# A maximum over partitions by two TensorE transposes instead of GpSimd's partition instruction

## The chip, the core and the metric

The kernel runs on one core of a Trainium2 chip. The metric is the time of one execution on the device in microseconds, the median of three runs. A core has five engines with a queue of instructions each: TensorE (PE in the rows: matrix products and transposes, results in PSUM banks), VectorE (DVE), ScalarE (ACT: functions by tables, copies), GpSimd (POOL) and SyncE (SP, which issues the transfers here).

## The reference

Linear attention with a softmax of q over the head dimension and of k over the tokens, and then two gated layers:

```python
k_s = k - np.max(k, axis=2, keepdims=True)          # k: 8 batches, 8 heads, 576 tokens, 64
k_s = np.exp(k_s)
k_s = k_s / (np.sum(k_s, axis=2, keepdims=True) + 1e-09)
kv = np.einsum('bhsd,bhse->bhde', k_s, v)
x = np.einsum('bhsd,bhde->bhse', q_s, kv)           # q_s: the same softmax over q's last axis
...                                                 # x becomes 4608 tokens x 512
x = (sigmoid(x @ w_gate) * (x @ w_val)) @ w_out     # d_ff 1536
h = x @ w_in                                        # d_ff 2048
g = (a[0] + a[1]*h + a[2]*h**2 + a[3]*h**3) / (1 + abs(b[0])*abs(h) + abs(b[1])*h**2 + 1e-6)
out = g @ w_out2
```

The maximum of k runs over the tokens, and in the kernel the tokens of a block lie on the 128 partitions: one maximum for each of the 128 columns of a pair of heads.

## The kernel before, in words

Tokens go in 9 blocks of 512 (`j`). The first layer is a loop over blocks and over 12 slices of the hidden dimension (`f`); one pass is a step. A step has on TensorE the front (`front_a`: 24 products of three-pass float32, into `pg` and `pv`) and the back of the step before (`back_a`: 12 products into four accumulators). ScalarE takes the sigmoid of `pg`, VectorE multiplies it with `pv` (`sg`), and the product is split in a high and a low part (`gh`, `gl`). The second layer follows in the same manner and reads the first layer's result from DRAM.

The attention of block `j` is spread over the steps of the block before, in four units (`u`, a pair of heads each). A unit at step `d` of its block (`UNIT_STEPS` 4, 6, 8, 10) has: at `d-4` the maximum of k over the 5 tokens of each partition (`att_km`, VectorE), then the maximum over the partitions (`partition_all_reduce` on GpSimd, `kma`) and the subtraction (`att_ks`, VectorE); at `d-3` the exponentials (`att_ke`, `att_qe`, ScalarE; they need another table than the sigmoid, so a table is loaded each way); at `d-2` the normalization of q (`att_n`, VectorE); at `d-1` the kv products (`att_kv`) and the four transposes of q (`att_q`); at `d` their product (`att_d`). The steps `d-1`, `d-3` are odd and `d`, `d-2`, `d-4` even, so two units share a step. The results of kv, of the transposes of q and of `att_d` rotate through the two PSUM banks of `ps_x`: each takes the bank of the one before the last, and waits until that has been read.

The opening is made otherwise: the first block's attention and layer, the second block's attention and the way in of the weights (float64 words, made float32 and split, on ScalarE, VectorE and GpSimd) are listed as operations with costs (`KINDS`), and a list scheduler (`in_time`) writes them out in the order that these costs suggest. The costs only set the order in each queue. In the opening most subtractions of k and q are on GpSimd, and so are the low parts of the weights (`wl`) and of `gl`.

Of the kernel before, what the change touches and what calls it, by code (L numbers as in the profile page):

```python
# [10 lines left out]
F32 = mybir.dt.float32  # L11
F32R = mybir.dt.float32r
U32 = mybir.dt.uint32
AF = mybir.ActivationFunctionType
# [5 lines left out]
P = 128  # L20
# [16 lines left out]

# The kinds of operations of the first block: engine, weight, table of the scalar engine. They only order the emission.
PE, ACT, DVE, POOL, DMA = "PE", "ACT", "DVE", "POOL", "DMA"
KINDS = {  # L40
    "load_k": (DMA, 0.92), "load_q": (DMA, 0.74), "load_v": (DMA, 0.92), "load_w": (DMA, 1.46), "load_ab": (DMA, 0.06),
    "k_max": (DVE, 0.73), "k_all": (POOL, 1.3), "k_sub": (POOL, 1.5), "k_exp": (ACT, 0.63, "exp"),
    "q_max": (DVE, 0.6), "q_sub": (POOL, 1.0), "q_exp": (ACT, 0.63, "exp"),
# [15 lines left out]
def in_time(ops, on_dve):  # L59
    """List scheduling: yields the operations in the order in which the engines can start them; an engine takes,  # L60
    of what is ready, the one with the longest rest behind it."""
    followers = {o: [] for o in ops}
# [42 lines left out]
def kernel(ctx: ExitStack, tc: tile.TileContext, q, k, v, w1, w2, ab_in, out):  # L105
    """Every float32 product is three float32r passes: an operand is H + L, where H is its value
    rounded to 12 bits and L the exact rest, and the product is H*H + L*H + H*L."""
    nc = tc.nc
# [49 lines left out]
    def order(last):  # L158
        """Four sums of three passes: those with the last operand to arrive at the end, or sum by sum."""
        return [(m, n) for m in range(4) for n in range(3)] if last else [(m, n) for n in range(3) for m in range(4)]  # L160

    stage = stage_ctx.enter_context(tc.tile_pool(name="stage", bufs=STAGES))

# [1 line left out]
    # in the order of their use: the last third of a step's with the next step's  # L165
    order1 = [x for f in range(NF1 + 1) for x in [(f, 0), (f, 1), (f - 1, 2)] if 0 <= x[0] < NF1]
# [21 lines left out]

    # float64 and float32 agree in the sign and in the exponent's top bit and low 7 bits for every
    # magnitude of float32; those beyond are first brought to the words of zero and infinity.  # L190
    def prep_bits_a(p):
# [22 lines left out]
    def prep(until, times=1):  # L214
        """Moves up to `until` pieces through the last stage, and those behind them one stage on."""
        for _ in range(times):
            jobs = []
            for n in (4, 3, 2, 1, 0):
                ready = done[n - 1] if n else len(pieces)
                if n == 0 and done[0] - done[3] >= STAGES:  # L220
                    continue
                if done[n] < min(ready, until + (4 if n == 0 else 3 if late_pool and n < 4 else 0)):
                    jobs.append((prep_load, prep_abs, prep_bits_a, prep_bits_b, prep_split)[n](done[n]))
                    done[n] += 1
            yield from mix(*[x for x in jobs if x])
# [9 lines left out]
    def run(*jobs):  # L235
        """Emits the jobs' operations in turn, so that an engine seldom waits for the operation before."""
        jobs = list(jobs)
        while jobs:
            for x in list(jobs):
                if next(x, jobs) is jobs:  # L240
                    jobs.remove(x)
# [6 lines left out]

# [1 line left out]
    att = att_ctx.enter_context(tc.tile_pool(name="att", bufs=2))  # L250
# [18 lines left out]
    def att_km(j, u):  # L269
        km = att.tile([P, P], F32, tag="km", name="km")  # L270
        nc.vector.tensor_reduce(out=km, in_=kt[j, u].rearrange("p c d -> p d c"), axis=AX.X, op=ALU.max)  # L271
        yield
        kmt[j, u] = att.tile([P, P], F32, tag="kma", name="kma")
        nc.gpsimd.partition_all_reduce(kmt[j, u], km, P, bass_isa.ReduceOp.max)  # L274

# [91 lines left out]

# [1 line left out]
    accs = {}  # L369
# [36 lines left out]

# [1 line left out]
    # The first block, with the weights' way in and the second block's attention: what each operation has to follow  # L408
    # because of its operands or of the room that it writes. Half of the first units use room that is free till then.
    free = x_raw.rearrange("p m c -> p (m c)")  # L410
# [9 lines left out]
    def chain(names, gen, *after):  # L420
        """Operations that a generator emits one after another."""
        for name in names:
            op(name, lambda: next(gen, None), *after)
            after = (name,)
# [9 lines left out]
    for i in range(2 * NHP):  # L434
# [8 lines left out]
        op(n("load_v"), partial(load_v, j, u), n("kv", 1 if j and u else 2), n("load_v", 1))  # L443
        chain([n("k_max"), n("k_all")], att_km(j, u), n("load_k"), n("k_max", 1), n("k_all", 2))
        also(n("k_all"), n("k_sub", 2), n("k_all", 1))
        op(n("k_sub"), partial(att_ks, j, u, pool_or_dve(n("k_sub"))), n("k_all"))
        op(n("q_max"), partial(att_qm, j, u), n("load_q"), n("q_max", 1), n("q_sub", 3))
# [8 lines left out]
        if j == 0:  # L456
            chain([n("x"), n("x_h"), n("x_l")], att_d(j, u), n("kv_l"), n("qt_l"))
            banks += [n("x")] if u == NHP - 1 else [("kv", 0, u + 1), ("qt", 0, u + 1), n("x")]
        else:
            chain([n("xa"), n("xa_out"), n("xb"), n("xb_out")], att_d(j, u), n("kv_l"), n("qt_l"),  # L460
                  *[("kv", 0, i) for i in range(1, NHP)])
            banks += [n("kv"), n("qt"), n("xa"), n("xb")]
    # the two rotating banks of the attention, in the order of their use
    last = {"kv": "kv_l", "qt": "qt_l", "x": "x_l", "xa": "xa_out", "xb": "xb_out"}
    for a, b in zip(banks, banks[1:]):
# [46 lines left out]

    work = {}

# [3 lines left out]
    for j in range(2, NBLK):  # L518
        for u in range(NHP):
# [4 lines left out]
            if j < B:  # L524
                at(d - 4, att_km, j, u)
                at(d - 4, att_ks, j, u, nc.vector)
                at(d - 3, att_ke, j, u)
                at(d - 3, load_v, j, u)
                at(d - 1, att_kv, j, u)
            at(d - 4, att_qm, j, u)  # L530
            at(d - 4, att_qs, j, u, nc.vector)
            at(d - 3, att_qe, j, u)
            at(d - 2, att_n, j, u, nc.vector)
# [15 lines left out]
    for i in range(NF1, NA):  # L549
# [11 lines left out]
        if f == NF1 - 1:  # L561
            split_x()
        want = 0
        if j == NBLK - 2:
# [4 lines left out]
        if pend:  # L569
            back_a(*pend.pop(0))  # L570
        pend.append((j, f))
        if j == NBLK - 1 and f == 4:
# [4 lines left out]

# [1 line left out]
    while done[4] < NW:  # L579
# [143 lines left out]
```

## Time and profile before

| what | us |
|---|---|
| median of three runs (1906.37 to 1907.53) | 1906.66 |
| span of the profiled execution, first to last instruction | 1899.6 |
| time of a run outside of that span | 7.1 |
| busy TensorE in the span | 1777.8 |
| busy VectorE, ScalarE, GpSimd | 1218.2, 997.4, 367.4 |

The profile shows one execution with the span given. Busy times are sums over the whole span; where an engine is full and where it waits is read from the stretches and timelines below.

### The profile page before, as it was taken

What the parts mean: (1) busy time and instruction counts of PE and PEld (TensorE: products, weight loads), DVE (VectorE), ACT (ScalarE), POOL (GpSimd) and SP (SyncE); (2) the same over time, 40 slices, a digit from 0 to 9 for tenths busy, and PEclk for the clock granted to TensorE, in tenths of its full rate; (3) what the DMA queues carried; (4) which work ended last, traced back from release to release, by engine and by line L of the source; (5) the groups of instructions that cost most, each with busy time, mean ns of one, the idle gap of its engine ahead of it and who ended that gap; (6) DMA issues with size and microseconds to landing.
All of it is one profiled execution on the core that took longest, in us unless ns stands there. A gap on an engine that the chain in (4) does not pass through costs nothing.

```text
span 1899.6 us, 21909 instructions
## 1 busy us (share of the span) xinstructions
PE 1777.8 (94%) x8320; PEld 1455.6 (77%) x8320; DVE 1218.2 (64%) x1867; ACT 997.4 (53%) x1622; POOL 367.4 (19%) x305
## 2 busy tenths in 40 slices
PE   1477699999999999999999899999999999999999
PEld 1356588888888888888887678888888888888887
DVE  4579344443435344443339998887888788888886
ACT  2345344243334344243334477777777777677765
POOL 2365300000000000000004532222222222222222
PEclk9979799999999999999999999999999999999999
DMA  4334111111102011121004510000000010000000
GB/s 151 114 114 144 46 62 40 42 60 35 46 21 81 20 62 40 42 86 39 11 12 159 173 56 23 23 23 23 23 23 34 11 45 23 23 23 23 1 23 23
DMA packets 39562, 95.96 MB, mean 51 GB/s; under 512 B 4128, under 2 KB 4128, under 8 KB 39456
## 3 DMA queue, kind: packets, MB, share of 16 engines
q1 hardware_dynamic: 39456, 94.55, 14.9%
q8 instruction: 65, 1.06, 0.2%
q14 instruction: 41, 0.34, 0.1%
HBM read 75.66 MB, written 18.87 MB: 50 GB/s over the span
## 4 chain that ended last, share of the span: by engine, by line
PE 83%; DVE 8%; issue 5%; POOL 2%; ACT 1%; DMA 0%; POOLq 0%; DVEq 0%; ACTq 0%; SPq 0%
PE accb L644 21%; PE acc L396 13%; PE ph L156 7%; PE ph L154 7%; PE ph L155 7%; PE pg L154 4%; PE pv L154 4%; PE pv L155 4%; PE pv L156 4%; PE pg L155 4%; PE pg L156 4%; DVE val L203 1%; DVE val L193 1%; DVE early L203 1%; PE ps_kv L315 1%
## 5 line engine op out<-in xcount | busy, mean ns | idle before, releaser
L147 POOL TENSOR_TENSOR glb<-gb,ghb 128x512 fp32r<-128x512 f32 x144 | 186.7, 1297 | 594.4 <-ACT ghb L145 594.4
L382 DVE TENSOR_TENSOR sg<-pv,sg 128x512 f32<-128x512 f32 x108 | 74.4, 689 | 350.6 <-PE pv L156 189.9
L380 ACT ACTIVATE sg<-pg 128x512 f32<-128x512 f32 x108 | 64.4, 596 | 349.8 <-PE pg L156 298.2
L154 PE MATMUL pv<-x_h,wh 128*128 128x512 f32 x432 | 173.3, 401 | 21.9 <-DVE sg L382 21.9
L612 ACT ACTIVATE h<-ph 128x512 f32<-128x512 f32 x144 | 86.2, 598 | 196.0 <-PE ph L156 194.7
L154 PE MATMUL pg<-x_h,wh 128*128 128x512 f32 x432 | 173.4, 401 | 15.3 <-ACT sg L380 15.0
L155 PE MATMUL pv<-x_h,wl 128*128 128x512 f32 x432 | 172.1, 398 | 10.0 <-POOL wl L147 10.0
L155 PE MATMUL pg<-x_h,wl 128*128 128x512 f32 x432 | 171.7, 398 | 0.0
L156 PE MATMUL pg<-x_l,wh 128*128 128x512 f32 x432 | 171.6, 397 | 0.0
L156 PE MATMUL pv<-x_l,wh 128*128 128x512 f32 x432 | 171.3, 397 | 0.0
L644 PE MATMUL accb<-wh,ghb 128*128 128x512 f32 x576 | 158.3, 389 | 0.0
L644 PE MATMUL accb<-wl,ghb 128*128 128x512 f32 x576 | 158.3, 389 | 0.0
L644 PE MATMUL accb<-wh,glb 128*128 128x512 f32 x576 | 158.3, 389 | 0.0
L274 POOL PARTITION_ALL_REDUCE kma<-km x32 | 24.7, 773 | 637.3 <-DVE km L271 593.0
L615 DVE SCALAR_TENSOR_TENSOR ah<-h,babs,ah 128x512 f32<-128x512 f32 x144 | 107.9, 749 | 53.8 <-ACT ah L613 53.8
L396 PE MATMUL acc<-gl,wh 128*128 128x512 f32 x432 | 122.3, 395 | 5.6 <-POOL gl L147 5.1
L154 PE MATMUL ph<-x_h,wh 128*128 128x512 f32 x320 | 124.6, 389 | 2.1 <-ACT x_h L145 2.1
L396 PE MATMUL acc<-gh,wh 128*128 128x512 f32 x432 | 124.4, 399 | 2.1 <-DVE x_raw L402 2.0
L644 PEld LDWEIGHTS accb<-wh,glb 128*128 128x128 f32 x576 | 108.2, 188 | 22.5
L644 PEld LDWEIGHTS accb<-wh,ghb 128*128 128x128 f32 x576 | 108.1, 188 | 22.5
L644 PEld LDWEIGHTS accb<-wl,ghb 128*128 128x128 f32 x576 | 108.1, 188 | 22.4
L156 PE MATMUL ph<-x_l,wh 128*128 128x512 f32 x320 | 124.6, 389 | 0.0
(111 smaller groups left out, 3980.2 us busy)
## 6 DMA issues: line engine op xcount, KB each, us to landing
raw<-in_w SPq DMA_DIRECT2D x68, 512.0 KB, 3.8
v<-in_v SPq DMA_DIRECT2D x30, 325.0 KB, 3.0
k<-in_k SPq DMA_DIRECT2D x30, 320.0 KB, 3.5
q<-in_q SPq DMA_DIRECT2D x36, 256.0 KB, 3.6
x<-x_raw SPq DMA_DIRECT2D x36, 256.0 KB, 2.3
x_raw<-x SPq DMA_DIRECT2D x9, 1024.0 KB, 5.5
out<-ob SPq DMA_DIRECT2D x36, 256.0 KB, 2.4
x_raw<-in_v SPq DMA_DIRECT2D x2, 325.0 KB, 4.5
```

Of the source, the lines that this page charges most:

```text
L147: lo_eng.tensor_tensor(out=lo, in0=src, in1=f32(h), op=ALU.subtract)
L154: nc.tensor.matmul(ps, wh, xh, start=first, stop=False)
L155: nc.tensor.matmul(ps, wl, xh, start=False, stop=False)
L156: nc.tensor.matmul(ps, wh, xl, start=False, stop=last)
L203: nc.vector.scalar_tensor_tensor(out=bits, in0=words[:, :, 0], scalar=29, in1=bits, op0=ALU.logical_shift_right, op1=ALU.bitwise_or)
L274: nc.gpsimd.partition_all_reduce(kmt[j, u], km, P, bass_isa.ReduceOp.max)
L380: nc.scalar.activation(sg, pg, AF.Sigmoid)
L382: nc.vector.tensor_tensor(out=sg, in0=pv, in1=sg, op=ALU.mult)
L396: nc.tensor.matmul(accs["a", j][m], x[:, m * P:(m + 1) * P], y, start=(f == 0 and n == 0), stop=(f == NF1 - 1 and n == 2))
L612: nc.scalar.activation(h2, ph, AF.Square)
L615: nc.vector.scalar_tensor_tensor(out=ah, in0=h2, scalar=babs[:, 1:2], in1=ah, op0=ALU.mult, op1=ALU.add)
L644: nc.tensor.matmul(accs["b", j][t], x[:, t * P:(t + 1) * P], y, start=(f == 0 and n == 0), stop=(f == NF2 - 1 and n == 2))
```

## The change

`partition_all_reduce` goes. `att_km` leaves the maximum per partition; `att_kt` transposes it on TensorE into a PSUM bank, takes the maximum over the columns on VectorE and writes it back over 128 columns; `att_kb` transposes that again, so that each partition has the maxima of all 128 columns, and ScalarE copies it to `kma`. In the loop of the steps `att_kt` stands just behind the front and the gating product of step `d-3` (`early_work`), `att_kb` behind the back (`late_work`); the subtraction follows there on GpSimd, and both exponentials go from `d-3` to `d-2`. 24 units (blocks 2 to 7) go through the loop, eight through the opening, where the scheduler gets the new operations and the banks that they use.

```diff
     def att_km(j, u):
         km = att.tile([P, P], F32, tag="km", name="km")
         nc.vector.tensor_reduce(out=km, in_=kt[j, u].rearrange("p c d -> p d c"), axis=AX.X, op=ALU.max)
+        kmt[j, u] = km
+
+    def att_kt(j, u, pool, tag):
+        ps = pool.tile([P, NB], F32, tag=tag, name="ps_kt")
+        nc.tensor.transpose(ps[:, :P], kmt[j, u], ident)
+        yield
+        mx = att.tile([P, 1], F32, tag="mx", name="mx")
+        nc.vector.tensor_reduce(out=mx, in_=ps[:, :P], axis=AX.X, op=ALU.max)
+        yield
+        nc.vector.tensor_copy(out=kmt[j, u], in_=mx.to_broadcast([P, P]))
+        yield
+
+    def att_kb(j, u, pool, tag):
+        ps = pool.tile([P, NB], F32, tag=tag, name="ps_kb")
+        nc.tensor.transpose(ps[:, :P], kmt[j, u], ident)
         yield
         kmt[j, u] = att.tile([P, P], F32, tag="kma", name="kma")
-        nc.gpsimd.partition_all_reduce(kmt[j, u], km, P, bass_isa.ReduceOp.max)
+        nc.scalar.activation(kmt[j, u], ps[:, :P], AF.Copy)
+        yield
...
-        chain([n("k_max"), n("k_all")], att_km(j, u), n("load_k"), n("k_max", 1), n("k_all", 2))
+        op(n("k_max"), partial(att_km, j, u), n("load_k"), n("k_max", 1), n("k_b", 2))
+        where = (ps_x, "x") if j else (ps_acc, "acc")
+        chain([n("k_t"), n("k_mx"), n("k_mb")], att_kt(j, u, *where), n("k_max"), n("k_mx", 2), n("k_t", 1))
+        chain([n("k_b"), n("k_cp")], att_kb(j, u, *where), n("k_mb"), n("k_cp", 2), n("k_b", 1))
...
                 at(d - 4, att_km, j, u)
-                at(d - 4, att_ks, j, u, nc.vector)
-                at(d - 3, att_ke, j, u)
+                early_work.setdefault(max(d - 3, NF1 + 1), []).append((att_kt, (j, u, ps_x, "x")))
+                late_work.setdefault(max(d - 3, NF1 + 1), []).append((att_kb, (j, u, ps_x, "x")))
+                late_work[max(d - 3, NF1 + 1)].append((att_ks, (j, u, nc.gpsimd)))
+                at(d - 2, att_ke, j, u)
...
-            at(d - 3, att_qe, j, u)
+            at(d - 2, att_qe, j, u)
...
+        run(sequence((), early_work.get(i, [])))
...
         run(prep(min(want, NW), 3), sequence(vec, work.get(i, [])))
         if pend:
             back_a(*pend.pop(0))
+        run(sequence((), late_work.get(i, [])))
```

What this does to the order of the queues, at three places. First GpSimd in the opening, from the end of its first memsets: before, with the maxima of the first four units (`ISA kma<-km`) and unnamed `ISA` rows between them and the subtractions (`k<-k,kma`, `x_raw<-x_raw,kma`, `q<-q,qs`):

```order
L274 ISA
L274 ISA kma<-km 128x128 x2
L290 ISA
L290 TENSOR_TENSOR k<-k,kma 128x640
L305 TENSOR_TENSOR q<-q,qs 128x512
L274 ISA
L274 ISA kma<-km 128x128
L290 ISA
L290 TENSOR_TENSOR x_raw<-x_raw,kma 128x640
```

and the same place after the change:

```order
L308 TENSOR_TENSOR k<-k,kma 128x640
L323 TENSOR_TENSOR q<-q,qs 128x512
L300 TENSOR_TENSOR q<-q,qm 128x512
L323 TENSOR_TENSOR q<-q,qs 128x512
L308 TENSOR_TENSOR x_raw<-x_raw,kma 128x640
```

The maxima and the unnamed rows beside them are gone; subtractions follow one another.

Second, TensorE in an odd step of the loop that has the kv products and the transposes of q of one unit (`ps_kv`, `ps_qt`) between the end of the front (`pv`) and the back (`acc`), before:

```order
L156 MATMUL pv<-x_l,wh 128x512
L315 MATMUL ps_kv<-v,k 64x65 [waits DMAHW6_49,Activation_49]
L315 MATMUL ps_kv<-v,k 64x65 x9
L339 MATMUL ps_qt<-ident,q 128x128 [waits DVE_49,Activation_49]
L339 MATMUL ps_qt<-ident,q 128x128 x3
L396 MATMUL acc<-gh,wh 128x512 x4
L396 MATMUL acc<-gh,wl 128x512 x4
L396 MATMUL acc<-gl,wh 128x512 x4
L154 MATMUL pg<-x_h,wh 128x512 [waits Activation_49]
```

and after:

```order
L157 MATMUL pv<-x_l,wh 128x512
L278 MATMUL ps_kt<-ident,km 128x128 [waits DVE_49,Activation_49]
L333 MATMUL ps_kv<-v,k 64x65 [waits DMAHW6_49,Activation_49]
L333 MATMUL ps_kv<-v,k 64x65 x9
L357 MATMUL ps_qt<-ident,q 128x128 [waits DVE_49,Activation_49]
L357 MATMUL ps_qt<-ident,q 128x128 x3
L414 MATMUL acc<-gh,wh 128x512 x4
L414 MATMUL acc<-gh,wl 128x512 x4
L414 MATMUL acc<-gl,wh 128x512 x4
L288 MATMUL ps_kb<-ident,km 128x128 [waits DVE_49,PE_49]
L155 MATMUL pg<-x_h,wh 128x512 [waits Activation_49]
```

The next unit's first transpose (`ps_kt`) stands ahead of kv and its second (`ps_kb`) behind the back, so three results come into the two rotating banks between the front and the back, and a fourth behind it.

Third, ScalarE over the exponentials of a unit and the next sigmoid (`sg<-pg`), before:

```order
L294 ACT_TABLE_LOAD
L294 ACTIVATE k<-k 128x640
L286 ACTIVATE q<-q 128x512 [waits DMAHW3_49]
L380 ACT_TABLE_LOAD [waits PE_49]
L380 ACTIVATE sg<-pg 128x512 [waits Activation_49]
```

and after:

```order
L312 ACT_TABLE_LOAD
L312 ACTIVATE k<-k 128x640 [waits Pool_49]
L304 ACTIVATE q<-q 128x512 [waits DMAHW0_49]
L398 ACT_TABLE_LOAD [waits DVE_49]
L398 ACTIVATE sg<-pg 128x512 [waits PE_49]
```

The exponentials stand a step later than before, the exponential of k waits for GpSimd, and the load of the sigmoid's table waits for VectorE where it waited for TensorE's front.

## Rows read from the trace of the kernel before

**Rows 1.** Stretches: us; busy time (instructions) of each engine; granted clock, DMA share, GB/s

```profile
0.00:240.00 240.00, 136.35 (x632) 103.91 (x633) 152.07 (x249) 95.74 (x158) 99.87 (x94) 0.89 0.35 112
60.00:240.00 180.00, 127.50 (x557) 97.42 (x558) 131.78 (x204) 82.95 (x137) 83.36 (x60) 0.85 0.33 104
300.00:400.00 100.00, 100.00 (x522) 82.58 (x521) 43.62 (x76) 35.76 (x59) 2.81 (x4) 1.00 0.12 39
```

**Rows 2.** TensorE's timeline, first front product and steady run: start, us, what

```profile
64.13 0.63 PE L154 MATMUL pg<-x_h,wh 128*128 128x512 f32 x1
...
239.59 1.09 PE L396 MATMUL acc<-gh,wh 128*128 128x512 f32 x4
```

**Rows 3.** Chain of waits to 250 us, first and last of eleven pieces

```profile
7.48 5.31 issue
...
218.16 6.67 issue
```

**Rows 4.** GpSimd's timeline in the opening; brackets: idle before, and releaser

```profile
21.34 1.52 POOL L290 TENSOR_TENSOR k<-k,kma 128x640 f32<-128x640 f32 x1 [7.11 <-issue]
29.75 0.72 POOL L274 PARTITION_ALL_REDUCE kma<-km  x1 [5.88 <-issue]
...
70.30 1.28 POOL L147 TENSOR_TENSOR wl<-early,wh 128x512 fp32r<-128x512 f32 x1 [3.34 <-ACT wh L145]
```

**Rows 5.** TensorE's timeline around steady steps

```profile
372.17 1.07 PE L396 MATMUL acc<-gh,wh 128*128 128x512 f32 x4
...
380.42 0.80 PE L315 MATMUL ps_kv<-v,k 128*64 128x65 f32 x20
381.16 0.66 PE L339 MATMUL ps_qt<-ident,q 128*128 128x128 f32 x4
381.57 1.18 PE L396 MATMUL acc<-gh,wh 128*128 128x512 f32 x4
382.59 1.08 PE L396 MATMUL acc<-gh,wl 128*128 128x512 f32 x4
...
384.43 0.39 PE L154 MATMUL pg<-x_h,wh 128*128 128x512 f32 x1
...
389.87 0.28 PE L154 MATMUL ps_xt<-qh,kvh 128*128 128x256 f32 x1
...
398.95 0.80 PE L315 MATMUL ps_kv<-v,k 128*64 128x65 f32 x20
```

**Rows 6.** Groups by line and shape: busy us, mean ns, idle before and releaser

```profile
L145 ACT ACTIVATE gh<-sg 128x512 fp32r<-128x512 f32 x108 | 68.0, 629 | 72.3 <-DVE sg L382 72.3
...
L290 POOL TENSOR_TENSOR k<-k,kma 128x640 f32<-128x640 f32 x5 | 7.7, 1533 | 20.7 <-issue 20.7
...
L365 ACT ACTIVATE x_raw<-ps_xt 128x128 f32<-128x128 f32 x8 | 2.1, 263 | 0.0
```

**Rows 7.** VectorE's timeline in the same steps

```profile
372.44 0.69 DVE L382 TENSOR_TENSOR sg<-pv,sg 128x512 f32<-128x512 f32 x1 [6.08 <-PE pv L156]
...
384.00 0.29 DVE L331 SCALAR_TENSOR_TENSOR kvl<-ps_kv,rs,kvh 64x64 fp32r<-64x64 f32 x1
...
393.35 0.68 DVE L299 TENSOR_REDUCE qs<-q 128x8 f32<-128x512 f32 x1
...
395.12 1.30 DVE L271 TENSOR_REDUCE km<-k 128x128 f32<-128x640 f32 x1
397.32 0.83 DVE L290 TENSOR_TENSOR k<-k,kma 128x640 f32<-128x640 f32 x1 [0.90 <-POOL kma L274]
...
399.38 0.68 DVE L382 TENSOR_TENSOR sg<-pv,sg 128x512 f32<-128x512 f32 x1
```

**Rows 8.** ScalarE's timeline in steps with exponentials

```profile
365.66 1.28 ACT L294 ACT_TABLE_LOAD   x1
...
368.23 1.28 ACT L380 ACT_TABLE_LOAD   x1
...
389.43 1.28 ACT L380 ACT_TABLE_LOAD   x1 [2.56 <-PE pg L156]
```

More of the change, by code (lines that the diff above doesn't have):

```diff
@@ L41 @@
     "load_k": (DMA, 0.92), "load_q": (DMA, 0.74), "load_v": (DMA, 0.92), "load_w": (DMA, 1.46), "load_ab": (DMA, 0.06),
-    "k_max": (DVE, 0.73), "k_all": (POOL, 1.3), "k_sub": (POOL, 1.5), "k_exp": (ACT, 0.63, "exp"),
+    "k_max": (DVE, 1.25), "k_t": (PE, 0.2), "k_mx": (DVE, 0.3), "k_mb": (DVE, 0.2), "k_b": (PE, 0.2),
+    "k_cp": (ACT, 0.33), "k_sub": (POOL, 1.5), "k_exp": (ACT, 0.63, "exp"),
     "q_max": (DVE, 0.6), "q_sub": (POOL, 1.0), "q_exp": (ACT, 0.63, "exp"),
@@ L443 @@
         op(n("load_v"), partial(load_v, j, u), n("kv", 1 if j and u else 2), n("load_v", 1))
-        chain([n("k_max"), n("k_all")], att_km(j, u), n("load_k"), n("k_max", 1), n("k_all", 2))
-        also(n("k_all"), n("k_sub", 2), n("k_all", 1))
-        op(n("k_sub"), partial(att_ks, j, u, pool_or_dve(n("k_sub"))), n("k_all"))
+        op(n("k_max"), partial(att_km, j, u), n("load_k"), n("k_max", 1), n("k_b", 2))
+        where = (ps_x, "x") if j else (ps_acc, "acc")
+        chain([n("k_t"), n("k_mx"), n("k_mb")], att_kt(j, u, *where), n("k_max"), n("k_mx", 2), n("k_t", 1))
+        chain([n("k_b"), n("k_cp")], att_kb(j, u, *where), n("k_mb"), n("k_cp", 2), n("k_b", 1))
+        also(n("k_cp"), n("k_sub", 2), n("k_cp", 1))
+        op(n("k_sub"), partial(att_ks, j, u, pool_or_dve(n("k_sub"))), n("k_cp"))
         op(n("q_max"), partial(att_qm, j, u), n("load_q"), n("q_max", 1), n("q_sub", 3))
@@ L458 @@
             banks += [n("x")] if u == NHP - 1 else [("kv", 0, u + 1), ("qt", 0, u + 1), n("x")]
+            banks += [("k_t", 1, u // 2), ("k_b", 1, u // 2)][:2 if u % 2 else 0]
         else:
@@ L461 @@
                   *[("kv", 0, i) for i in range(1, NHP)])
-            banks += [n("kv"), n("qt"), n("xa"), n("xb")]
-    last = {"kv": "kv_l", "qt": "qt_l", "x": "x_l", "xa": "xa_out", "xb": "xb_out"}
+            banks += [n("kv"), n("qt")]
+            banks += [("k_t", 1, u + 2), ("k_b", 1, u + 2)] if u < 2 else []
+            banks += [n("xa"), n("xb")]
+    last = {"k_t": "k_mx", "k_b": "k_cp", "kv": "kv_l", "qt": "qt_l", "x": "x_l", "xa": "xa_out", "xb": "xb_out"}
     for a, b in zip(banks, banks[1:]):
@@ L511 @@
         ops[o][0]()
-    work = {}
+    work, early_work, late_work = {}, {}, {}
     def at(step, fn, *args):
```

## The prediction

> **What bounds the kernel now.** I read the table by stretches first. Between 300 and 400 us TensorE is busy all the time, and the second layer looks alike; up to 240 us it is busy for 136 us, and no other engine is full either: VectorE 152, ScalarE 96, GpSimd 100 [rows 1]. So the kernel has two regimes. In the opening, where the first block, the weights and the attention of two blocks are worked on together, something makes everybody wait. From about 239.6 us on, where the run of back products begins [rows 2], only TensorE's own work counts.
>
> The chain of waits says what the opening waits for: "issue", time in which the engine on the chain waited for nothing that the profile shows. Eleven such pieces, from 7.48 to 224.83 us, stand beside a GpSimd instruction: 5.31, 2.27, 1.19, 6.72, 5.72, 7.60, 6.21, 6.11, 5.54, 6.79 and 6.67, in all 60.1 us [rows 3]. GpSimd's timeline names the place: the gap is there each time GpSimd goes from the partition maximum to an ordinary subtraction (7.11 ahead of 21.34) or back (5.88 ahead of 29.75), fourteen times in the opening, while the maximum itself takes 0.72 [rows 4]. The emitted order has an unnamed ISA row at each of these places, and no other engine's result is late there. I read the gap as the price of changing GpSimd's code.
>
> **The change, part by part.** *Removed in the opening.* GpSimd keeps one kind of work. The eleven gaps on the chain (60.1) go, and the five maxima that the chain passes, 0.72 each, 3.6: 63.7 us.
>
> [...]
>
> *Added in the opening.* In place of one maximum come five steps over three engines: transpose, maximum over columns, copy, transpose, copy out. Prices: four transposes of this size take 0.41 (381.16 to 381.57), so 0.10 each, and the change of number format back to the big products costs 0.10 (the first four of them take 1.18 instead of 1.08), as much assumed on the way in: 0.30 for a transpose that stands alone, 0.10 for one beside others [rows 5]. The maximum of 128 PSUM columns is not in the trace: a quarter of the reduction over 512 (0.68) is 0.17, the whole 0.68 [rows 7]; I take 0.28. The broadcast copy lies below the copy of 128 x 128 out of PSUM on ScalarE, 0.26; I take 0.20, and 0.26 for ScalarE's own [rows 6]. Sum 0.30 + 0.28 + 0.20 + 0.30 + 0.26 = 1.34. The old path has a wait of 0.90 round a maximum of 0.72 [rows 4, 7], about 0.10 per hand-over; four more make 1.74. Five units' maxima stand on the chain: 8.7 us. The opening then gains 63.7 - 8.7 = 55.0 us.
>
> Bounds of that. Which wait comes next? VectorE is busy 131.8 of the 180 us from 60 to 240, TensorE 127.5 [rows 1], and the first front product is at 64.13 [rows 2]. Six of the gaps, 28.8 us, lie before it, so it moves to some 36. From there VectorE's work alone would end at 36 + 132 + 4 (sixteen small instructions) = 172, TensorE's, if a third of its 52 us of idle time there stays, at 36 + 128 + 17 = 181, against 240: 59 to 68 less. So the 55 isn't cut by the next engine, and 66 is the upper end. The lower, 40, is where the gaps of the second half only uncover half of other waits.
>
> *Added in the steady steps.* 24 units (blocks 2 to 7, four pairs of heads) each put two transposes on TensorE, which has no free time. Eighteen of the first transposes stand just ahead of the kv products (second order fence), in the same number format, 0.10; six stand alone, 0.30; all 24 second ones stand between two runs of big products, 0.30. That is 18 x 0.40 + 6 x 0.60 = 10.8 us; at 0.10 for all 48 it is 4.8.
>
> [...]
>
> *A new wait in the steady steps.* The attention's products share two PSUM banks in turn. In the eighteen steps the first transpose now takes one, kv the other, and the transposes of q need the first again: they wait until VectorE has taken its maximum. VectorE comes to that only after the gating product (`sg`), which starts 0.27 after the front's end (372.17 to 372.44) and takes 0.69; with 0.28 and 0.10 the bank is free at 1.34 [rows 5, 7]. TensorE is there after 0.20 + 0.74 (kv) = 0.94 [rows 5]. Wait 0.40, times 18: 7.2 us.
>
> Two moved steps decide whether it stays at 0.40. The exponentials go one step later, so the load of the sigmoid's table now falls in these steps. In the trace a load can stand ahead of the wait for the front (368.23, no idle time before it) or behind it (389.43, after 2.56 of idle time until TensorE's product, with the sigmoid 1.28 late) [rows 8]; the emitted order has it behind a wait on VectorE alone now (third fence), so it is hidden. And VectorE must be free: in the step before, it now waits for the exponential of q. From that front's end: gating product to 0.96, ScalarE's copy of it 0.63 [rows 6] to 1.7, two copies of x at about 0.26 [rows 6] to 2.3, load and both exponentials 2.57 (365.66 to 368.23) [rows 8] to 4.9, VectorE's normalization 1.77 to 6.8, and the rest to the next gating product 4.26 less the 0.90 and 0.83 that leave, to 9.3 [rows 7]. The next front ends at 9.08 (389.87 to 398.95) [rows 5], its gating product is due at 9.35. It just fits; every 0.1 us that it misses costs 1.8 us.
>
> *Moved, at no cost.* The subtraction of the maximum goes from VectorE to GpSimd, 1.53 each [rows 6]; GpSimd has nothing else in these steps and the exponential is a step away. If that cover were gone, 0.7 us more per unit would fall on the exponentials. The ScalarE copy runs under the next front. No transfer changes its place past the wait of another.
>
> **The sum.** -55.0 + 10.8 + 7.2 = -37.0. The profiled execution has a span of 1899.6; 7.1 us round it make the median of 1906.66, and I leave these as they are. Forecast: 1869.7, said as **1870 us**.
>
> **Rivals.**
> *The opening has a second brake.* Only the gaps ahead of the first front count: 28.8 + 2.2 (three maxima) - 7.0 (four new paths) = 24 of gain, less 18: 1901 us. For it: VectorE has the most work of the opening, 152 us. Against it: 48 us of its idle time lie between 60 and 240, and 52 of TensorE's [rows 1].
>
> *The sigmoid comes late in the eighteen steps* (table load behind the front, or VectorE behind by as much). The wait becomes 0.40 + 1.28 = 1.7, 30 us in all: -55 + 10.8 + 30 = -14, 1893 us. Against it stands the order; for it, the fit without slack.
>
> *Slower: the second transpose waits for its bank.* It needs kv's bank, and so the split of kv. That ends at 384.29 in the step shown, 0.14 ahead of the next front at 384.43 [rows 5, 7]; VectorE's two new instructions can make it 0.48 later, TensorE comes 0.60 later, so 0.26 are left. A delay there holds the whole next front. The kernel is no faster once the wait is 37 / 18 = 2.1 us in each of the eighteen steps, that is once the split is 2.4 us later than I reckon; at 3.5 it is 1870 + 18 x 3.24 = 1928 us. For it: the split passes ScalarE and VectorE twice. Against: both are idle for over half of such a step [rows 1].
>
> *The gaps are not code changes* but belong to GpSimd's first instruction after a pause. Then they stay, and only 18 us are added: 1925 us. Against it: an ordinary instruction of GpSimd after 3.34 us without work was released by ScalarE, with no gap behind that (70.30) [rows 4].
>
> **How the numbers follow.** A difference below 0.2% (3.8 us) is about what cannot be told from no change here. Chances: the forecast with its own bounds (1850 to 1886) 0.75; quicker than that 0.03; second brake 0.08, of which 0.02 within 0.2%; late sigmoid 0.07; bank of kv 0.04, of which 0.01 within 0.2%; gaps stay 0.03. The sum's bounds are -66 + 5 = -61 (1846) and -40 + 25 = -15 (1892). The range 1848 to 1892 leaves out the slow cases, most of the second brake, and a little below. Faster 0.91, same 0.03, slower 0.06.
>
> **What would show it.** Right: GpSimd's timeline without gaps of 5 us and more between its instructions up to the first back products; the first front product near 36 us and the steady run near 185; eighteen idle pieces of about 0.4 us of TensorE ahead of the transposes of q, released by VectorE's maximum, and steps with attention 0.8 us longer. Wrong: "issue" beside GpSimd still on the chain, VectorE full through the opening, or the waits of the transposes at 1 us and more each.

## The result, and the profile after

The changed kernel takes **1856.61 us** (median of four runs, 1856.32 to 1857.73) against 1907.1 on the same chip before: ratio 0.9736, interval 0.9722 to 0.975, so 50 us faster. The span of its profiled execution is 1854.6 us.

By stretches, as in [rows 1] (us; busy time and instructions of TensorE, its weight loads, VectorE, ScalarE, GpSimd; granted clock, DMA share, GB/s):

```profile
0.00:180.00 180.00, 135.02 (x641) 101.36 (x642) 161.98 (x261) 96.84 (x162) 103.66 (x86) 0.93 0.47 150
60.00:180.00 120.00, 97.70 (x451) 74.85 (x450) 107.00 (x156) 67.54 (x109) 72.39 (x46) 0.90 0.41 124
300.00:400.00 100.00, 99.00 (x522) 81.53 (x521) 40.94 (x80) 37.47 (x63) 6.28 (x4) 1.00 0.14 48
```

TensorE does in 180 us what took 240. VectorE is busy for 107 of the 120 us from 60 to 180, where it was for 131.8 of 180. From 300 to 400 us TensorE is no longer full: 1.0 us is idle.

TensorE's timeline, the first front product and the start of the run of back products, as in [rows 2]:

```profile
34.62 0.79 PE L155 MATMUL pg<-x_h,wh 128*128 128x512 f32 x1
...
181.24 1.07 PE L414 MATMUL acc<-gh,wh 128*128 128x512 f32 x4
```

29.5 us are gained ahead of the first front (64.13 to 34.62) and 28.8 between it and the steady run (175.5 to 146.6): the opening is 58.3 us shorter. GpSimd's timeline in it, as in [rows 4]:

```profile
10.12 1.69 POOL L308 TENSOR_TENSOR k<-k,kma 128x640 f32<-128x640 f32 x1 [6.48 <-ACT kma L291]
13.20 1.04 POOL L323 TENSOR_TENSOR q<-q,qs 128x512 f32<-128x512 f32 x1 [1.39 <-DVE rs L338]
...
17.81 1.54 POOL L308 TENSOR_TENSOR x_raw<-x_raw,kma 128x640 f32<-128x640 f32 x1 [0.84 <-ACT kma L291]
...
30.93 1.26 POOL L148 TENSOR_TENSOR wl<-early,wh 128x512 fp32r<-128x512 f32 x1 [6.70 <-ACT wh L146]
```

The long gaps now have another engine behind them, as releaser; the gaps of 5.8 to 9.0 us with "issue" behind them are gone. On the chain of waits no piece of "issue" stands ahead of a GpSimd instruction any more; most of the chain up to the steady run is VectorE's work, with some 25 us of "issue" left on it in pieces below 2 us.

What the loop of steps costs more is read from SyncE's timeline, at the store of the first block's result and at that of the seventh block, behind the last step that carries one of the 24 units. Before:

```profile
250.90 6.40 SPq L405 DMA_DIRECT2D x<-x_raw  x4
...
892.29 3.06 SPq L405 DMA_DIRECT2D x<-x_raw  x3
```

and after:

```profile
192.56 5.24 SPq L423 DMA_DIRECT2D x<-x_raw  x4
...
847.00 2.97 SPq L423 DMA_DIRECT2D x<-x_raw  x3
```

641.39 us before, 654.44 after: 13.05 more. TensorE's timeline in one of the eighteen steps, as in [rows 5]:

```profile
343.72 0.27 PE L278 MATMUL ps_kt<-ident,km 128*128 128x128 f32 x1
343.92 0.80 PE L333 MATMUL ps_kv<-v,k 128*64 128x65 f32 x20
345.02 0.63 PE L357 MATMUL ps_qt<-ident,q 128*128 128x128 f32 x4 [0.30 <-DVE mx L281]
345.41 1.18 PE L414 MATMUL acc<-gh,wh 128*128 128x512 f32 x4
...
348.26 0.27 PE L288 MATMUL ps_kb<-ident,km 128*128 128x128 f32 x1
348.29 0.48 PE L155 MATMUL pg<-x_h,wh 128*128 128x512 f32 x1
```

VectorE's timeline there, as in [rows 7]:

```profile
343.16 0.69 DVE L300 TENSOR_TENSOR q<-q,qm 128x512 f32<-128x512 f32 x1
343.99 0.69 DVE L400 TENSOR_TENSOR sg<-pv,sg 128x512 f32<-128x512 f32 x1
344.60 0.28 DVE L281 TENSOR_REDUCE mx<-ps_kt 128x1 f32<-128x128 f32 x1
344.91 0.23 DVE L283 COPY km<-mx 128x128 f32<-128x128 f32 x1
```

and what TensorE's transposes of q waited for in the whole loop (us in all, times):

```profile
  DVE mx L281: 6.0, 18
```

The wait is where it was foreseen: 0.33 each, eighteen times, for VectorE's maximum. VectorE ends its subtraction of q at 343.85, 0.14 ahead of the gating product: it just fits. ScalarE's table load, as in [rows 8], lies under the front and not behind it:

```profile
339.46 1.28 ACT L398 ACT_TABLE_LOAD   x1
343.23 0.60 ACT L398 ACTIVATE sg<-pg 128x512 f32<-128x512 f32 x1 [2.49 <-PE pg L157]
```

### The profile page after: what moved, and what is told of

Same layout as the page of the kernel before. It is cut to its first block, busy times and chain, and to the rows that moved or that the text cites. A ratio compares the mean times of both kernels' runs of the same rounds, so it can differ in the third digit from the quotient of the medians.

```text
span 1854.6 us, 22112 instructions
## 1 busy us (share of the span) xinstructions
PE 1783.7 (96%) x8384; PEld 1458.1 (79%) x8384; DVE 1224.2 (66%) x1907; ACT 1007.9 (54%) x1656; POOL 392.1 (21%) x297
## 4 chain that ended last, share of the span: by engine, by line
PE 83%; DVE 12%; issue 3%; ACT 2%; DMA 1%; POOL 0%; DVEq 0%; ACTq 0%; SPq 0%
PE accb L672 21%; PE acc L414 13%; PE ph L155 7%; PE ph L157 7%; PE ph L156 7%; PE pv L155 4%; PE pv L157 4%; PE pg L155 4%; PE pv L156 4%; PE pg L156 4%; PE pg L157 4%; DVE sg L400 1%; DVE early L207 1%; DVE val L194 1%; DVE early L204 1%
## 5 line engine op out<-in xcount | busy, mean ns | idle before, releaser
L308 POOL TENSOR_TENSOR k<-k,kma 128x640 f32<-128x640 f32 x29 | 46.4, 1600 | 599.2 <-ACT kma L291 599.2
L659 DVE SCALAR_TENSOR_TENSOR u<-ah,r 128x512 f32<-128x512 f32 x144 | 99.4, 690 | 39.5 <-ACT r L649 39.5
```

Of the source, the lines that this page charges most:

```text
L308: eng.tensor_tensor(out=t, in0=t, in1=kmt[j, u].unsqueeze(1).to_broadcast([P, KCH, P]), op=ALU.subtract)
L659: nc.vector.scalar_tensor_tensor(out=u, in0=ah, scalar=q_one, in1=r, op0=ALU.add, op1=ALU.mult)
```

## The experiments

Times are medians; the kernel before took 1908.0 to 1908.6 beside them. "End of the opening" is the start of ScalarE's operation on the second layer's coefficients (`babs`), which stands once in the program, behind the sigmoid of the loop's first step: 248.77 before, 190.43 after.

**The opening alone.** The loop keeps GpSimd's maximum (`att_kr` is the old `att_km`).

```diff
-                at(d - 4, att_km, j, u)
-                early_work.setdefault(max(d - 3, NF1 + 1), []).append((att_kt, (j, u, ps_x, "x")))
-                late_work.setdefault(max(d - 3, NF1 + 1), []).append((att_kb, (j, u, ps_x, "x")))
-                late_work[max(d - 3, NF1 + 1)].append((att_ks, (j, u, nc.gpsimd)))
-                at(d - 2, att_ke, j, u)
+                at(d - 4, att_kr, j, u)
+                at(d - 4, att_ks, j, u, nc.vector)
+                at(d - 3, att_ke, j, u)
```

> The opening as changed, the loop of the steps as before (GpSimd's maximum, VectorE's subtraction, exponentials at d-3). Theory: the whole gain is the opening's 58 us and the loop's part of the change costs 13 us, so this runs 13 us below the changed kernel, 1844 us, with one change of GpSimd's code ahead of the loop's first maximum and one behind its last, both beside other work. Rival, the loop gains too (VectorE freed, no hand-over to GpSimd): 1857 us or more. The 5.5 us by which the time fell more than the span: they go with the opening's code changes if the time here is about 2 us above the span, with any use of the partition instruction if it is about 7 us above it (then 1849 us).

1843.56 us, ratio 0.9663 (0.9648 to 0.9677), 13.05 less than the changed kernel. SyncE's two stores:

```profile
194.12 5.90 SPq L430 DMA_DIRECT2D x<-x_raw  x3
...
835.51 3.46 SPq L430 DMA_DIRECT2D x<-x_raw  x4
```

641.39 us again. All of the gain is the opening's, and the loop's part of the change only costs. The profiled run took 1844.33 us with a span of 1842.5, so 1.8 lie outside. But the runs of the kernel before that stand beside it lie 1.8 to 2.1 above their spans as well (1905.15 with 1903.2, 1910.26 with 1908.2). So the 7.1 us that the table of before puts outside the span belong to that one profile, and to neither part of the change.

**The loop alone.** The converse: the opening as before, the loop as changed (`att_km2` is the new `att_km`).

```diff
-                at(d - 4, att_km, j, u)
-                at(d - 4, att_ks, j, u, nc.vector)
-                at(d - 3, att_ke, j, u)
+                at(d - 4, att_km2, j, u)
+                early_work.setdefault(max(d - 3, NF1 + 1), []).append((att_kt, (j, u, ps_x, "x")))
+                late_work.setdefault(max(d - 3, NF1 + 1), []).append((att_kb, (j, u, ps_x, "x")))
+                late_work[max(d - 3, NF1 + 1)].append((att_ks, (j, u, nc.gpsimd)))
+                at(d - 2, att_ke, j, u)
```

> The opening as before, the loop as changed. Theory: the span of the kernel before and 13 us, 1913, the time 1920 us if what lies outside the span stays at 7.5, 1915 us if it falls to 2. Rival, the loop's part is neutral: 1907 us.

1918.25 us, ratio 1.006 (1.0043 to 1.0077). From first to last store it is 654.46 us, so 13.07 more, while the median is 10.2 more. Its opening is that of before and ended at 251.63, 2.9 later than in the profile of before: the same opening differs by so much between executions. The changed opening does too: it ended at 190.43 in the changed kernel and at 192.00 in the opening-alone kernel.

**Idle maxima.** Changed kernel, with a partition maximum that nobody reads ahead of seven of GpSimd's subtractions of k in the opening.

```diff
+        if j < 2 and eng is nc.gpsimd:
+            spare = att.tile([P, D], F32, tag="spare", name="spare", bufs=1)
+            nc.gpsimd.partition_all_reduce(spare, kmt[j, u][:, :D], P, bass_isa.ReduceOp.max)
         eng.tensor_tensor(
             out=t, in0=t, in1=kmt[j, u]
```

> The changed kernel with seven partition maxima put back on GpSimd in the opening, each ahead of a subtraction, half as wide (64 of 128 columns), into a tile that nothing reads. Theory, the price is the change of GpSimd's code: fourteen changes of 5 to 8 us each, most of them on the chain as before, so 40 to 75 us more than the changed kernel, near 1912 us, with gaps of 5 to 8 us on both sides of each maximum. Rival, the old path was long by the maximum itself and its place between two engines: seven times 0.8 us at most, 1862 us, and no gaps.

1932.02 us (1931.52 to 1935.32), 75.4 more than the changed kernel; the opening ends at 269.87. GpSimd's timeline:

```profile
23.24 1.52 POOL L311 TENSOR_TENSOR k<-k,kma 128x640 f32<-128x640 f32 x1 [7.09 <-issue]
...
35.99 0.54 POOL L310 PARTITION_ALL_REDUCE spare<-kma  x1 [7.83 <-issue]
...
212.60 0.54 POOL L310 PARTITION_ALL_REDUCE spare<-kma  x1 [5.90 <-issue]
...
220.55 1.52 POOL L311 TENSOR_TENSOR k<-k,kma 128x640 f32<-128x640 f32 x1 [7.41 <-issue]
```

and GpSimd's group of these maxima up to 300 us (count, busy, mean ns, idle before):

```profile
L310 POOL PARTITION_ALL_REDUCE spare<-kma x7 | 4.2, 604 | 50.7 <-issue 50.7
```

Seven instructions of 0.60 bring fourteen gaps, ahead of each and behind each: thirteen of 5.9 to 8.6, and one of 11.74 ahead of the first maximum, which includes the start of the program. This settles when the gaps come: with the change between the maximum and ordinary work, though no result of the maximum is waited for. What GpSimd does in such a gap no row shows; "change of code" stays a reading. The loss is larger than the 58 gained, I think because here the change back stands behind the path of the transposes; no run shows that apart.

**Maximum first.** Changed kernel, with VectorE's maximum ahead of the gating product (its copy stays behind it), so that the bank is free when q's transposes come.

```diff
         vec = vec_a(j, f, *ps)
         next(vec)
+        early = sequence((), early_work.get(i, []))
+        next(early, None)
+        next(early, None)
         next(vec)
...
-        run(sequence((), early_work.get(i, [])))
+        run(early)
```

> The changed kernel with VectorE's maximum of the first transpose ahead of the gating product in the loop, where it stood behind it. Theory: the eighteen waits of q's transposes (0.33 us each) go, 6 us less: 1851 us. Rival: the time goes into the next wait, because the gating product comes later and the bank of kv then holds the second transpose: 1857 us.

1852.67 us, ratio 0.9712 (0.9698 to 0.9727). The loop is 650.90, 3.5 of the 6.0 us shorter. TensorE's timeline:

```profile
345.51 0.66 PE L357 MATMUL ps_qt<-ident,q 128*128 128x128 f32 x4
...
347.86 1.07 PE L414 MATMUL acc<-gl,wh 128*128 128x512 f32 x4
348.91 0.30 PE L288 MATMUL ps_kb<-ident,km 128*128 128x128 f32 x1
```

The transposes of q (345.51) wait no more. The second transpose now starts 1.05 behind the last group of the back, where it was 0.91 (347.35 to 348.26): 0.14, times eighteen 2.5 us, which are the rest. Its bank is that of kv. VectorE's timeline has the end of kv's split, later now with the gating product, and that of TensorE's weight loads the load of the transpose right behind it:

```profile
348.19 0.58 DVE L349 SCALAR_TENSOR_TENSOR kvl<-ps_kv,rs,kvh 64x64 fp32r<-64x64 f32 x2 [0.76 <-ACT kvh L345]
```

```profile
348.88 0.14 PEld L288 LDWEIGHTS ps_kb<-ident,km 128*128 128x128 f32 x1 [0.38 <-issue]
```

The split ends at 348.77 and the load starts at 348.88, with 0.38 of idle time that the profile gives to no engine. I read the bank from these times.

**Transposes twice.** Each of the loop's 48 transposes is issued twice, the second into columns that nobody reads.

```diff
         nc.tensor.transpose(ps[:, :P], kmt[j, u], ident)
+        if j > 1:
+            nc.tensor.transpose(ps[:, P:2 * P], kmt[j, u], ident)
```

> The changed kernel with each of the loop's 48 new transposes made twice, the second time into columns of the same bank that nothing reads. Theory, a transpose that stands beside another costs its 0.10 us: 5 us more than the changed kernel, 1861 us. Rival, 0.275 us each: 13 us more, 1870 us.

1860.96 us (1859.36 to 1862.47), 4.35 more; the loop is 3.8 longer. TensorE's timeline in one of the eighteen steps, and what the transposes of q waited for in the whole loop:

```profile
346.30 0.27 PE L278 MATMUL ps_kt<-ident,km 128*128 128x128 f32 x1
346.41 0.27 PE L280 MATMUL ps_kt<-ident,km 128*128 128x128 f32 x1
```

```profile
  DVE mx L283: 4.0, 18
```

The wait for VectorE's maximum is 4.0 us in all, where it was 6.0: eighteen of the added transposes lie in time that TensorE lost before. So the added work is 3.8 + 2.0 = 5.8 us for 48, 0.12 each, and the rows agree with 0.11 from one start to the next. The rival's 0.275 us is near what one transpose lasts in the rows (0.27), but not what a further one adds.

**GpSimd keeps the maxima alone.** The kernel before, with the opposite cure: all ordinary work of GpSimd in the opening goes to VectorE, in the planner's costs too.

```diff
-    "w_h": (ACT, 0.52), "w_l": (POOL, 1.23),
+    "w_h": (ACT, 0.52), "w_l": (DVE, 0.6),
...
-        yield from split_steps(*wt[p], val.pop(p), nc.gpsimd)
+        yield from split_steps(*wt[p], val.pop(p), nc.vector if p < NW1 else nc.gpsimd)
...
-    on_dve = {("k_sub", 0, 0)} | {("q_sub", *x) for x in Q_SUB_ON_DVE}
+    on_dve = {(w, j, u) for w in ("k_sub", "q_sub") for j in range(2) for u in range(NHP)}
```

(and in the same way `q_div` and `g_l`)

> The kernel before with its partition maxima on GpSimd, but with all of the opening's ordinary GpSimd work (subtractions of k and q, divisions of q, low parts of the weights and of g: 64 instructions, 83 us there) on VectorE instead, which does them in about half the time. Theory, the price is the change of code and not the maximum: GpSimd changes its code once before its first maximum and once behind the last, so the opening loses its gaps although the maxima stay. VectorE then has its 152 us, less what GpSimd's instructions stretch (some 30), and 45 more: the steady run begins near 190 to 200 instead of 249, 1850 to 1860 us. Rival, the maximum's place between two engines makes the opening long: no faster than before, 1907 us or, with VectorE's added work, more.

1830.56 us, ratio 0.9591 (0.9578 to 0.9604): 26 us below the changed kernel, better than I expected by 20 to 30. The opening ends at 179.17. GpSimd's only change of this kind in the opening stands at the start:

```profile
13.53 1.43 POOL L274 PARTITION_ALL_REDUCE kma<-km  x2 [9.65 <-issue]
```

That the gaps are gone is only a part of it. VectorE's groups up to 180 us (count, busy, mean ns), in the changed kernel:

```profile
L207 DVE SCALAR_TENSOR_TENSOR early<-raw,early 128x512 uint32<-128x512 uint32 x34 | 34.3, 1015 | 0.0
L194 DVE TENSOR_SCALAR early<-early 128x512 f32<-128x512 f32 x34 | 24.2, 718 | 0.0
L400 DVE TENSOR_TENSOR sg<-pv,sg 128x512 f32<-128x512 f32 x11 | 7.5, 680 | 3.7 <-ACT sg L398 3.7
```

and in this one:

```profile
L206 DVE SCALAR_TENSOR_TENSOR early<-raw,early 128x512 uint32<-128x512 uint32 x34 | 22.7, 685 | 0.0
L193 DVE TENSOR_SCALAR early<-early 128x512 f32<-128x512 f32 x34 | 14.1, 423 | 2.3 <-ACT early L187 2.3
L382 DVE TENSOR_TENSOR sg<-pv,sg 128x512 f32<-128x512 f32 x13 | 8.9, 686 | 5.5 <-ACT babs L558 3.5 <-ACT sg L380 1.9
```

The same operations on the same shapes take 0.69 and 0.42 where they took 1.02 and 0.72; the gating product, one of whose operands is in PSUM, takes 0.68 and 0.69. How that comes about is in the changed kernel's timelines, VectorE's:

```profile
109.25 1.49 DVE L197 TENSOR_SCALAR early<-early 128x512 uint32<-128x512 uint32 x1
...
113.89 0.41 DVE L197 TENSOR_SCALAR early<-early 128x512 uint32<-128x512 uint32 x1
```

and GpSimd's:

```profile
108.78 1.68 POOL L148 TENSOR_TENSOR gl<-sg,gh 128x512 fp32r<-128x512 f32 x1
```

An operation of 0.41 lasts 1.49 where an instruction of GpSimd lies beside it until 110.46, and ends 0.28 behind that: I read this as an operation that is held, and not slowed as a whole. The durations bear it out: but for a few they are 0.37 to 0.43 or 1.43 to 1.53. A line's own view (ns: least, median and most) shows the two ends, for line 194 in the changed kernel:

```profile
L194 DVE TENSOR_SCALAR early<-early x34: 366/416/1670, 22.8 to 145.3; 128x512 f32<-128x512 f32 x34
```

and for the kernel of the next experiment, with nothing on GpSimd:

```profile
L194 DVE TENSOR_SCALAR early<-early x34: 411/420/428, 27.8 to 144.0; 128x512 f32<-128x512 f32 x34
```

The medians agree; the mean was raised by those that met GpSimd.

**Nothing on GpSimd.** The opening-alone kernel with the same moves to VectorE.

```diff
-        yield from split_steps(*wt[p], val.pop(p), nc.gpsimd)
+        yield from split_steps(*wt[p], val.pop(p), nc.vector if p < NW1 else nc.gpsimd)
...
-        chain([n("q_sum"), n("q_add"), n("q_inv"), n("q_div")], att_n(j, u, nc.gpsimd), n("q_exp"), n("q_sum", 1), n("q_div", 2))
+        chain([n("q_sum"), n("q_add"), n("q_inv"), n("q_div")], att_n(j, u, nc.vector), n("q_exp"), n("q_sum", 1), n("q_div", 2))
```

> The opening of the opening-only kernel (maxima by two transposes) with all of GpSimd's ordinary work of the opening moved to VectorE, as in the kernel that gave GpSimd the maxima alone; the loop keeps GpSimd's maximum. GpSimd has nothing in the opening. Theory (two brakes that add: code changes, and VectorE's operations stretched by GpSimd beside them): VectorE's two bit operations stay at 0.42 us, and the 8 us by which the maxima-alone kernel begins its first front product later (42.87 against 34.62) are saved too: 1822 us, 1818 to 1827. First rival (the opening now ends by the total work of VectorE, to which the transposes add two small steps a unit): 1830 to 1836. Second rival (what the maxima-alone kernel gained was the shorter path of GpSimd's maximum against the transposes, not the stretching): 1843 us and more, as the opening-only kernel.

1827.83 us (1826.55 to 1829.91), ratio 0.9586 (0.9569 to 0.9603): the lowest median, 15.7 below the opening-alone kernel, from which it differs in who does the ordinary work and in the order that the scheduler makes of that. The second rival falls, and the theory isn't met in full: the first front comes at 40.05, 2.8 earlier than with the maxima alone and not 8, and the opening ends at 174.81, 4.4 earlier. VectorE is busy for 163.15 of its first 180 us, against 157.87 there, as the first rival said. By the medians the two kernels lie 2.7 us apart, and their intervals overlap: with nothing else on GpSimd in the opening, it hardly matters there whether GpSimd's instruction or the two transposes make the maximum.

**Idle work on GpSimd.** The kernel before this one, with unread work of one kind on GpSimd, so without a change from maxima to ordinary work in the opening.

```diff
+        if p < NW1:
+            spare = att.tile([P, 96], F32, tag="spare", name="spare", bufs=1)
+            nc.gpsimd.tensor_copy(out=spare, in_=f32(wt[p][0][:, :96]))
+            for _ in range(10):
+                nc.gpsimd.tensor_tensor(out=spare, in0=spare, in1=spare, op=ALU.subtract)
```

> The kernel before this one in the list, and behind each weight piece of the opening eleven small GpSimd operations (128 x 96, a copy and ten subtractions of a tile from itself) that nobody reads; all of one kind, so no change of code. Theory (GpSimd's work stretches VectorE's operations beside it, 35 us for about 100 us of GpSimd work in the changed kernel): VectorE's bit operations rise from 0.42 towards 0.7 us, and the time goes up by 15 to 35 us. Rival (VectorE's durations have another cause, such as the order): they stay at 0.42 us, and the time stays within 3 us.

1906.76 us, 79 more and far beyond both. The opening itself ends 17.4 later, at 192.18, within what the theory said, with the bit operations at 0.52 and 0.78; the other 62 are another thing. GpSimd's timeline:

```profile
247.04 4.16 POOL L218 TENSOR_TENSOR spare<-spare 128x96 f32<-128x96 f32 x10
256.94 0.72 POOL L304 PARTITION_ALL_REDUCE kma<-km  x1 [5.75 <-issue]
```

and TensorE's:

```profile
260.50 1.39 PE L426 MATMUL acc<-gh,wh 128*128 128x512 f32 x2 [59.56 <-DVE x_raw L432]
```

The idle work ran late (to 251.2), and the loop's first maximum stood behind it in GpSimd's queue. So its time doesn't answer the question, and it was asked again with less:

```diff
-            for _ in range(10):
+            for _ in range(4):
```

> The kernel with idle GpSimd operations, with four subtractions behind each copy in place of ten, so that GpSimd (36 x 2.3 = 83 us of unread work at 0.48 us each) keeps up with the weight pieces and the first maximum of the loop doesn't stand behind a row of idle work (which held TensorE for 60 us in the kernel with ten). There the opening itself, up to the last operation of it on ScalarE, ended 17.4 us later than without idle work (192.2 against 174.8), with 130 us of GpSimd work up to 180 us. Theory (stretching in proportion to GpSimd's work): 17.4 x 83 / 130 = 11 us, the bit operations near 0.48 and 0.73 us, the time 1839 (1834 to 1844), nothing lost behind the opening. Rival (the loss needs GpSimd's queue to run late): within 3 us of 1828.

1837.08 us (1836.54 to 1837.51), 9.25 more; the opening ends 10.3 later, at 185.12, and nothing is lost behind it. VectorE's groups:

```profile
L207 DVE SCALAR_TENSOR_TENSOR early<-raw,early 128x512 uint32<-128x512 uint32 x34 | 24.2, 726 | 0.0
L194 DVE TENSOR_SCALAR early<-early 128x512 f32<-128x512 f32 x34 | 16.9, 503 | 0.2 <-ACT early L188 0.2
```

0.42 has become 0.50 and 0.68 has become 0.73, with work on GpSimd that nobody waits for, and with the same instructions on VectorE. That is the theory's case. GpSimd is busy for 102 of the first 180 us here and for 104 in the changed kernel; the opening-alone kernel has the same opening, and there it is 17.2 longer than with nothing on GpSimd. By that, some 10 of the 17.2 would be of this kind, an estimate; what the other 7 are was not separated.

## Why the prediction came out as it did

1870 us was forecast, with a range of 1848 to 1892; it is 1856.6. The mechanism held, and the 13.4 us between lie in three places: the opening, the loop, and the time around the span.

**The gaps.** Right, and shown: those of 5.8 to 9.0 us vanish when the maxima go or when the ordinary work goes, and come back with seven maxima that nobody reads. The rival by which they follow a pause falls: behind a maximum they come without one (23.24 in the idle-maxima kernel), and the changed kernel has a pause of 6.70 us with no such gap behind it (30.93). That it is code that changes was the prediction's word for it, and no row shows that.

**The opening, -55.0.** It was 58.3. The first front was foreseen near 36 and came at 34.6, the steady run near 185 and came at 181.2, inside the bounds of 40 to 66. The price of a new path was too low, though: the maximum of 128 columns takes 0.28 as taken, but the transposes of the first five units take 0.42 to 0.48 for 0.30, the copy 0.45 in the mean of the opening for 0.20 (0.23 is the median of all 32), and with the waits between the pieces such a unit needs 2.8 to 4.8 us from the start of its first transpose to the end of the copy out, where 1.74 was reckoned. That the sum is off by 3.3 all the same means that part of this lies beside other work, or that more than the eleven gaps was won; the runs don't split it, and to that extent the nearness is luck.

No second brake cut the gain, though VectorE, busy for 162 of the first 180 us, is not far from the "full" that was to show one. A brake was there all the same, in a form that I hadn't thought of: VectorE held by GpSimd. Moving the work away shortens the opening by some 17 us (192.0 in the opening-alone kernel, 174.8 with nothing on GpSimd), some 10 of them for this reason by the estimate above. It was there before too, as VectorE's groups up to 240 us show for the kernel before:

```profile
L206 DVE SCALAR_TENSOR_TENSOR early<-raw,early 128x512 uint32<-128x512 uint32 x34 | 27.8, 820 | 0.0
L193 DVE TENSOR_SCALAR early<-early 128x512 f32<-128x512 f32 x34 | 22.6, 663 | 6.2 <-ACT early L187 6.2
```

So it stands on both sides of the sum.

**The transposes in the steady steps, +10.8.** The term was mis-sized. With the wait taken off, 13.05 less 6.0 leaves 7.05 for 48, 0.15 each, where I had 0.10 for eighteen and 0.30 for thirty. The doubled transposes put one beside another at 0.12, near the 0.10 taken, so what a lone one pays to be between other products is about 0.03, by difference, not the 0.20 that I assumed for two changes of number format.

**The new wait, +7.2.** Right in place, count and releaser: 18 times 0.33, 6.0 us, for 0.40. Putting VectorE's maximum first takes it away and gives 2.5 of 6.0 back at kv's bank: the mechanism of the rival that ends slower is there, with 0.14 a step, far from the 2.1 that it needed.

**The moved steps at no cost.** Right: the table load is hidden, VectorE fits with 0.14 to spare, the late-sigmoid rival didn't occur.

**The 7.1 us around the span.** Wrong. The timed runs of the changed kernel have their own spans: 1856.38 for the one of 1854.6, so 1.8 us lie around it. The rest, 5.3, is that the profiled execution of before was a quick one: its span of 1899.6 lies below every span of the later runs of that kernel (1902.3 to 1908.8), and the same opening ended 2.9 later in the loop-alone kernel. By the two profiles the gain is 45.0 us, by the medians 50.5. Which stretch has the other 2.4 stays open.

3.3 (opening) + 5.0 (loop) + 5.3 (the quick execution) make 13.6, for the 13.4 to be explained. The last of the three has nothing to do with the mechanism.

## What to carry to other kernels

Where GpSimd alternates between its partition instruction and ordinary arithmetic, count the alternations and not the instructions: each cost some 6 to 9 us of GpSimd's time here, and it was enough to give it one kind of work, whichever. Where VectorE is the busiest engine, work that is put on GpSimd to spare it can be paid back in VectorE's longer operations (0.42 became 0.72 here, in the mean): moved to VectorE, it made the two best of these kernels, one of them with GpSimd's maxima kept, 26 us faster than the change that this document is about. Where TensorE was full, as in the loop, a GpSimd instruction off the path was better than two cheap transposes on it (641.39 us against 654.44), so the change is worth making in the opening at most.

## What the runs showed of the hardware

In the opening, many operations of VectorE that had an instruction of GpSimd beside them lasted longer. In the changed kernel the `TENSOR_SCALAR` of line 194, with one operand in SBUF, has a median of 0.42 us, a mean of 0.72 and a longest of 1.67; with nothing on GpSimd its longest is 0.43. The mean of line 207, with two operands in SBUF, is 1.02, and 0.68 with nothing on GpSimd. The gating product, with an operand in PSUM, stayed at 0.67 to 0.69 in the changed kernel, and the reductions of q, with their one operand in SBUF, at 0.67 in the mean. One of each lay wholly beside an instruction of GpSimd, by GpSimd's timeline:

```profile
35.05 1.22 POOL L323 TENSOR_TENSOR q<-q,qs 128x512 f32<-128x512 f32 x1
...
148.24 1.29 POOL L323 TENSOR_TENSOR q<-q,qs 128x512 f32<-128x512 f32 x1 [4.38 <-DVE qs L321]
```

and VectorE's:

```profile
35.29 0.67 DVE L296 TENSOR_REDUCE qm<-q 128x8 f32<-128x512 f32 x1
...
148.55 0.68 DVE L400 TENSOR_TENSOR sg<-pv,sg 128x512 f32<-128x512 f32 x1
```

What sets these operations apart no row shows. VectorE's means in the profile of before (0.66 for the operation of line 193, whose median is 0.42) were already a sign of the second gain.
